# Attention's side work dealt by counts, its output product on VectorE, and 12 instead of 8 of 32 weight jobs in the MoE

## The chip, the cores and the metric

One core of a Trainium2 chip. The metric is the device time of one execution in microseconds.

## The reference, cut to what matters

```python
def _attn_ref(q, k, v, w1, b1, w2):          # q, k, v: 4 x 8 x 576 x 64
    scores = scale * np.matmul(q, k.transpose(0, 1, 3, 2))
    ...                                      # bias: 8 tables over (i, j), one a head, from a small net
    scores = scores + bias.transpose(2, 0, 1)[None, :, :, :]
    attn = np.exp(scores - np.max(scores, axis=-1, keepdims=True))
    attn = attn / (np.sum(attn, axis=-1, keepdims=True) + 1e-09)
    return np.matmul(attn, v)

def _moe_ref(x, w_in, w_out, a, b):          # x: 2304 x 512, w_in: 512 x 2048, w_out: 2048 x 512
    h = x @ w_in
    P = a[0] + a[1] * h + a[2] * h ** 2 + a[3] * h ** 3
    Q = 1.0 + np.abs(b[0]) * np.abs(h) + np.abs(b[1]) * h ** 2
    return (P / (Q + 1e-06)) @ w_out
```

The output of attention, with its heads side by side, is the x of the second part. The weights come as 64-bit floating point numbers.

## The kernel before

There are three stages, each written out as a Python loop; every engine runs its instructions in the order in which they are written.

**Bias.** 36 row groups make the bias tables and store them in DRAM.

**Attention.** A unit is a pair of heads and a batch entry: 16 units, of five steps each. Step c of a unit takes 128 rows of the queries for both heads (c = 0 to 3), or the last 64 rows of both together (c = 4). `step_a(i)` issues step i's scores (`e_qk`, TensorE, into two tiles of PSUM that are used in turn), then ScalarE's exponential for the second head of the step before, then transposes of the probabilities of two steps before (`e_tp`, `e_tail`; ScalarE copies them out of PSUM), then some keys of PV (`e_pv`), then VectorE's copy of the scores with bias and minimum (`e_ttr`, L349, called the masked copy here; it frees the scores' PSUM). PV of a unit is done in two halves of its queries; each half has five keys (four of 128 keys for both heads and a last one), which come into the list `fill` at places 1 and 4, counted by the unit of the step two behind. Before, a step takes three from `fill` where more than four are in it, and two otherwise. `e_pvout` copies a finished half out of PSUM. `load_rb` fetches the factors (one over the row sum, spread over partitions) from DRAM, and `e_norm`, the output product, multiplies a unit by them and stores it in DRAM (`xd`).

**Weight jobs.** TensorE multiplies in a 32-bit format that keeps fewer bits, so each weight is split into a high and a low part. 32 jobs (16 column blocks f of two matrices) do this: `load` (two DMAs of 512 KB, `wx` and `wy`), VectorE `mag`, `tail`, `sign`, `power`, `low`, ScalarE `rebias`, and `store` (two DMAs of 256 KB). `w_load` later reads the parts back into SBUF. Before, 24 jobs stand in a list `bg`, the load of the job after next behind each store, and `step_a` takes as many entries of it as keep it even over the steps: some 198 entries over 71 steps, 2.8 a step. The other 8 (`LATE = 4` blocks) run in the MoE.

**MoE.** 48 steps; step s has 384 tokens and 256 of the hidden columns, 24 matmuls for h (`mm1`) and, for step s - 2, 18 for the output (`mm2`). In between, ScalarE, GpSimd and VectorE form the rational function (`rat0`, `rat1`, `dv0` to `dv4`, `pl1`). The first half of the steps uses hidden columns 0 to 1023, the second half the rest, whose weights are read in at steps 20 to 25. `job(s, stage)` puts a weight job into every second step, from step `J0` on. h lies in the same two PSUM tiles as the scores did; `dv1` frees them. The output product of the last unit stands between the stages.

## Time and profile before

| | |
|---|---|
| median of 3 runs | 773.12 us (764.43 to 775.09) |
| profiled execution | 770.95 us |
| its span | 769.2 us |
| bias stage, up to about | 62 us |
| attention, up to about | 357 us |
| MoE | the rest |

The span is the time from the first to the last recorded instruction; the profiled execution has 1.8 us around it. Busy time of an engine is the sum of its recorded instructions; matmuls overlap, so a TensorE that is always busy may still be held up, and where it is shows in the time from one start to the next. Idle time is given with what ended it.

### The profile page before, as it was taken

Reading aid. Unit: us, or ns where it says so; the run is one execution under the profiler, and the core shown is the slowest. Engines: PE = TensorE matmul, PEld = TensorE weight load, DVE = VectorE, ACT = ScalarE, POOL = GpSimd, SP = SyncE. Lnnn points to the kernel's source line nnn. Section 1 sums busy time; section 2 is a strip of 40 time slices with the busy share of each in tenths; the row PEclk is TensorE's granted clock in tenths of the full one; section 3 lists DMA queues with packets and bytes.
Section 4 is the critical chain, followed back from the end, with each engine's and each line's share of the span. In section 5 each row is a group of like instructions: output and inputs, shape, how many; then the busy total and the mean of one; then the engine's idle time right before and its main releaser. Section 6 shows DMA issues by size and latency. Waiting matters only on the chain.

```text
span 769.2 us, 12185 instructions
## 1 busy us (share of the span) xinstructions
PE 738.1 (96%) x4210; PEld 561.5 (73%) x4210; DVE 572.2 (74%) x963; ACT 516.1 (67%) x965; POOL 204.3 (27%) x122
## 2 busy tenths in 40 slices
PE   6899999999999989999799999999999999999997
PEld 2236666655665656667788998998998899899896
DVE  7995766756667647563789999998776878687766
ACT  5978878766786767785657767666666656655552
POOL 0000000000000000000545444534533443443452
PEclk9999999989999999999999999999999999999999
DMA  4888788888879868954515263515853121230121
GB/s 135 295 289 280 233 278 273 294 274 268 272 251 286 273 226 285 302 181 138 179 43 164 83 193 111 188 69 171 237 187 117 42 82 52 72 124 17 65 83 41
DMA packets 107420, 137.66 MB, mean 179 GB/s; under 512 B 17104, under 2 KB 66528, under 8 KB 107360
## 3 DMA queue, kind: packets, MB, share of 16 engines
q1 hardware_dynamic: 106768, 136.11, 54.3%
q8 instruction: 33, 0.54, 0.3%
q10 hardware_dynamic: 592, 0.78, 0.3%
q14 instruction: 27, 0.22, 0.1%
HBM read 94.96 MB, written 41.90 MB: 178 GB/s over the span
## 4 chain that ended last, share of the span: by engine, by line
PE 79%; DMA 4%; DVE 3%; ACT 3%; issue 2%; POOL 1%; SPq 0%; DVEq 0%; POOLq 0%
PE o L749 26%; PE h L313 25%; PE sc L338 11%; PE tp L416 8%; PE pv L449 7%; PE pv L454 2%; DVE s L349 1%; DMA wx<-in_w_out_dram 1%; DMA k<-in_kt_dram 1%; ACT p L367 1%; PE pv L431 1%; DMA ws<-wh 1%; ACT ptm L511 1%; DVE wh L152 1%; DMA xr<-xd 0%
## 5 line engine op out<-in xcount | busy, mean ns | idle before, releaser
L679 POOL TENSOR_TENSOR u<-u,w 128x768 f32<-128x768 f32 x48 | 93.7, 1951 | 197.6 <-ACT u L677 189.1
L349 DVE CUSTOM_DVE_ANT_0 s<-sc,bias 128x576 f32<-128x576 f32 x144 | 103.7, 752 | 45.3 <-PE sc L338 40.4
L367 ACT ACTIVATE p<-s,m 128x576 f32<-128x576 f32 x144 | 112.8, 783 | 12.7 <-DVE m L349 12.4
L511 ACT COPY ptm<-tp 128x512 f32<-128x512 f32 x144 | 78.4, 588 | 58.6 <-PE tp L416 57.6
L400 POOL TENSOR_TENSOR xs<-xs,rb 128x576 f32<-128x576 f32 x16 | 23.6, 1473 | 341.7 <-DMA rb<-rs 191.3
L676 ACT ACTIVATE w<-h 128x768 f32<-128x768 f32 x48 | 39.1, 814 | 103.4 <-PE h L313 102.0
L338 PE MATMUL sc<-k,q 64*128 64x288 f32 x512 | 95.4, 442 | 11.0 <-DVE m L349 9.6
L313 PE MATMUL h<-xh,wg 128*128 128x384 f32 x384 | 102.6, 338 | 0.0
L718 POOL TENSOR_TENSOR gl<-m,r 128x768 fp32r<-128x768 f32 x47 | 87.2, 1854 | 13.7 <-DVE m L711 13.7
L338 PEld LDWEIGHTS sc<-k,q 64*128 64x128 f32 x512 | 51.2, 189 | 48.0 <-DVE m L349 23.5
L416 PEld LDWEIGHTS tp<-ident,p 128*128 128x128 f32 x576 | 65.5, 145 | 27.9 <-issue 8.9
L416 PE MATMUL tp<-ident,p 128*128 128x128 f32 x576 | 82.5, 286 | 0.0
L687 DVE TENSOR_TENSOR t<-t,h 128x768 f32<-128x768 f32 x48 | 45.7, 952 | 46.0 <-ACT t L678 28.1
L749 PE MATMUL o<-wg,gh 128*128 128x512 f32 x288 | 79.0, 391 | 0.0
L449 PE MATMUL pv<-ptm,v 128*64 128x320 f32 (+1 forms) x512 | 77.9, 427 | 0.0
L683 ACT ACTIVATE r<-u,qc 128x768 f32<-128x768 f32 x48 | 45.1, 940 | 42.6 <-POOL u L679 42.6
L313 PEld LDWEIGHTS h<-xh,wg 128*128 128x128 f32 x384 | 70.5, 190 | 1.1
L711 DVE SCALAR_TENSOR_TENSOR m<-t,cst,m 128x768 f32<-128x768 f32 x48 | 64.1, 1336 | 1.7
L313 PE MATMUL h<-xh,wih 128*128 128x384 f32 x192 | 64.9, 338 | 0.0
L313 PE MATMUL h<-xl,wg 128*128 128x384 f32 x192 | 64.8, 338 | 0.0
L313 PE MATMUL h<-xh,wil 128*128 128x384 f32 x192 | 64.7, 337 | 0.0
L313 PE MATMUL h<-xl,wih 128*128 128x384 f32 x192 | 64.6, 336 | 0.0
(77 smaller groups left out, 1390.6 us busy)
## 6 DMA issues: line engine op xcount, KB each, us to landing
tab<-e SPq DMA_DIRECT2D x36, 295.5 KB
wx<-in_w_in_dram SPq DMA_DIRECT2D x16, 512.0 KB
wy<-in_w_in_dram SPq DMA_DIRECT2D x16, 512.0 KB
wx<-in_w_out_dram SPq DMA_DIRECT2D x16, 512.0 KB
wy<-in_w_out_dram SPq DMA_DIRECT2D x16, 512.0 KB
ws<-wh SPq DMA_DIRECT2D x32, 256.0 KB
ws<-wl SPq DMA_DIRECT2D x32, 256.0 KB
wg<-ws SPq DMA_DIRECT2D x32, 256.0 KB
```

Of the source, the lines that this page charges most:

```text
L313: T.matmul(hps[s][:, j, :TT], w[:, k, sl], x[:, k, :], start=(k == 0 and z == 0), stop=(k == KD - 1 and z == 2),)
L338: T.matmul(sc[i, j][:, a, :SH], l, k[r, o + a * SH:o + (a + 1) * SH], start=True, stop=True,)
L349: V.tensor_tensor_reduce(out=t.rearrange("p (a s) -> p a s", a=2), in0=sc.pop((i, j))[:, :, :SH], in1=bias[p][:, idx, :].rearrange("p (a s ...
L367: A.activation(out=prob[i][:, z * S:z * S + S], in_=t, func=AF.Exp, bias=m, scale=-1.0, accum_out=ssum[u][:, k:k + 1],)
L416: T.transpose(ps[:, kc, :], prob[i][:, k0:k0 + P], ident)
L449: T.matmul(ps[64 * j:64 * j + 64, :w], v[:, kc, 64 * j:64 * j + 64], ptm[u, hf][:, kc, j, :w], start=(kc == 0), stop=False,)
L511: A.copy(out=o, in_=x)
L679: G.tensor_tensor(out=u, in0=u, in1=w, op=ALU.mult)
L687: V.tensor_tensor(out=rt[s, "t"], in0=rt[s, "t"], in1=hps[s][:, :, :TT], op=ALU.mult)
L711: V.scalar_tensor_tensor(out=m, in0=rt[s, "t"], scalar=abs_[:, 0:1], in1=m, op0=ALU.add, op1=ALU.subtract)
L718: eng.tensor_tensor(out=lo, in0=rt[s, "m"], in1=rt[s, "r0"], op=ALU.mult)
L749: T.matmul(po[n, c], l[:, j, c * P:(c + 1) * P], r[fp][:, j, :], start=(first and x is a), stop=(last and x is z),)
```

## The change

In attention each step takes a fixed number of PV keys (`PV_KEYS`) and of VectorE's job instructions (`JOB_OPS`), by its place in the unit two steps behind. The list of a job's entries is made anew (`in_order`): the load of the job after next stands behind `sign`, and `rebias` is put aside (`actq`) and issued early in ScalarE's part of the next step. The reciprocal of the row sums stands behind the masked copies, and `e_pvout` behind the jobs. The output product moves from GpSimd to VectorE and, for units 0 to 14, from place 3 of the next unit to place 0 of the one after it. In the MoE `LATE = 6` leaves 12 jobs, one every second step as before, from step 1 on; 20 stay in attention. Their order is changed so that both blocks of a pair come together.

```diff
@@ -75,7 +75,7 @@
     wih, wil, woh, wol = {}, {}, {}, {}
     wide = w_in.dtype != F32
     KH = KF // 2
-    LATE = 4
+    LATE = 6
 
     def w_alloc(pool, g):
         for d_, nm in ((wih, "wih"), (wil, "wil")):
@@ -193,14 +193,16 @@
     def w_job(f, part):
         return w_conv(f, part) if wide else w_plain(f, part)
 
-    def ahead(jobs, after=()):
-        seq = [j[0] for j in jobs[:2]]
-        for i, (_, *stages) in enumerate(jobs):
-            for st in stages:
-                seq += st
+    def in_order(jobs, after):
+        seq = [("sp", j[0]) for j in jobs[:2]]
+        for i, (_, first, act, last) in enumerate(jobs):
+            *vec, store = last
+            seq += [("dve", x) for x in first[:1]] + [("act", x) for x in act]
+            seq += [("dve", x) for x in first[1:] + vec[:1]]
             if i + 2 < len(jobs):
-                seq.append(jobs[i + 2][0])
-            seq += after.get(i, [])
+                seq.append(("sp", jobs[i + 2][0]))
+            seq += [("dve", x) for x in vec[1:]] + [("sp", store)]
+            seq += [("sp", x) for x in after.get(i, [])]
         return seq
 
     def w_hilo(f, part):
@@ -397,7 +399,7 @@
             def e_norm(u):
                 x = xs.pop(u)
                 p, b = units[u]
-                G.tensor_tensor(out=x, in0=x, in1=rb.pop(u), op=ALU.mult)
+                V.tensor_tensor(out=x, in0=x, in1=rb.pop(u), op=ALU.mult)
                 nc.sync.dma_start(out=xd[b][:, p, :], in_=x)
 
             def half(c):
@@ -473,6 +475,22 @@
             fill = []
             NU = len(units)
             TL = 2
+            PV_KEYS = (2, 3, 1, 2, 2)
+            JOB_OPS = (1, 2, 2, 1, 1)
+            actq = []
+
+            def run_act():
+                while actq:
+                    actq.pop(0)()
+
+            def run_jobs(n):
+                while bg and (n > 0 or bg[0][0] != "dve"):
+                    kind, fn = bg.pop(0)
+                    if kind == "act":
+                        actq.append(fn)
+                    else:
+                        fn()
+                    n -= kind == "dve"
 
             def step_a(i):
                 def ok(d):
@@ -502,21 +520,22 @@
                 if ok(1):
                     for j in heads(i - 1)[1:]:
                         e_exp(i - 1, j)
-                    if steps[i - 1][1] == 4:
-                        e_recip(steps[i - 1][0])
+                run_act()
                 if ok(TL):
                     hs = heads(i - TL)
                     for j in hs:
                         for o, x in e_tp(i - TL, j):
                             A.copy(out=o, in_=x)
                     tails, fin = e_tail(i - TL)
-                for _ in range((3 if len(fill) > 4 else 2) if i < NS + TL else len(fill)):
+                for _ in range(PV_KEYS[(i - TL) % 5] if i < NS + TL else len(fill)):
                     if fill:
                         e_pv(*fill.pop(0))
                 if ok(0):
                     for j in heads(i):
                         e_ttr(i, j)
                     e_exp(i, heads(i)[0])
+                if ok(1) and steps[i - 1][1] == 4:
+                    e_recip(steps[i - 1][0])
                 if ok(TL):
                     for o, x in tails:
                         A.copy(out=o, in_=x)
@@ -533,15 +552,14 @@
                     w_load(KH - 1, 0)
                 if i == NS + 1:
                     load_x(1, 1)
-                want = min(2, max(0, i - 3)) if i < 5 else 2 + (i - 4) * (nbg - 2) // (NS - 9)
-                e_pvout()
                 u2, c2 = divmod(i - TL, 5)
+                if c2 == 0 and 1 < u2 <= NU:
+                    e_norm(u2 - 2)
                 if c2 == 0 and 0 < u2 <= NU:
                     load_rb(u2 - 1)
-                if c2 == 3 and 0 < u2 <= NU:
-                    e_norm(u2 - 1)
-                while bg and nbg - len(bg) < want:
-                    bg.pop(0)()
+                if i >= 2:
+                    run_jobs(JOB_OPS[c2] if i >= 3 else 0)
+                e_pvout()
 
             with ExitStack() as bctx:
                 tpool = bctx.enter_context(tc.tile_pool(name="tpool", bufs=1, side="right"))
@@ -595,11 +613,10 @@
                     after[2 * (f + 2) + 1] = [lambda f=f: [w_load(f, z) for z in range(2)]]
                 for f in range(4, 6):
                     after[2 * f + 5] = [lambda f=f: [w_load(f, z) for z in range(2)]]
-                after[18] = [lambda: w_carve(1)]
+                after[16] = [lambda: w_carve(1)]
                 for f in range(2, 4):
-                    after[18 + f] = [lambda f=f: [w_load(f, z) for z in range(2)]]
-                bg = ahead(bg, after)
-                nbg = len(bg)
+                    after[15 + f] = [lambda f=f: [w_load(f, z) for z in range(2)]]
+                bg = in_order(bg, after)
 
                 for n in range(LEAD):
                     relu(n)
@@ -651,7 +668,8 @@
             for i in range(EARLY, NS + TL + 1):
                 step_a(i)
             while bg:
-                bg.pop(0)()
+                run_act()
+                run_jobs(1)
             while fill:
                 e_pv(*fill.pop(0))
             e_pvout()
@@ -778,8 +796,10 @@
 
             for f in range(KH - 2, KH):
                 w_load(f, 1)
-            jobs = [w_job(f, y) for f in range(KF - LATE, KF) for y in range(2)]
-            J0 = FPR
+            jobs = [
+                w_job(f + j, y) for f in range(KF - LATE, KF, 2) for y in range(2) for j in range(2)
+            ]
+            J0 = 1
             for x in jobs[:2]:
                 x[0]()
```

The lines of the changed kernel are up to 20 further down (L338 is L340, L349 is L351, L400 is L402, L687 is L705). In the rows below the number in a name is the step (`sc31_0`: scores of step 31, head 0) or the unit (`pv5_0`: PV of unit 5, half 0), and the last number only tells buffers apart.

TensorE's queue in attention, from the scores of step 31 to those of step 32 (`tp29` and `tt29` are the transposes of step 29), before:

```order
L338 MATMUL sc31_0_1982<-k6_1752,q6_1751 128x288
L338 MATMUL sc31_1_1983<-k6_1752,q6_1751 128x288
L338 MATMUL sc31_0_1982<-k6_1752,q6_1751 128x288
L338 MATMUL sc31_1_1983<-k6_1752,q6_1751 128x288
L416 MATMUL tp29_2_1989<-ident_60,p29_1922 128x128 x4
L434 MATMUL tt29_1995<-ident_60,p29_1922 128x128
L435 MATMUL tt29_1995<-ident_60,p29_1922 64x128
L378 MATMUL tt29_1995<-ident_60,sum5_1735 9x128
L338 MATMUL sc32_0_2024<-k6_1752,q6_1751 128x288
L338 MATMUL sc32_1_2025<-k6_1752,q6_1751 128x288
```

and now:

```order
L340 MATMUL sc31_0_1965<-k6_1737,q6_1736 128x288
L340 MATMUL sc31_1_1966<-k6_1737,q6_1736 128x288
L340 MATMUL sc31_0_1965<-k6_1737,q6_1736 128x288
L340 MATMUL sc31_1_1966<-k6_1737,q6_1736 128x288
L418 MATMUL tp29_2_1972<-ident_60,p29_1903 128x128 x4
L436 MATMUL tt29_1978<-ident_60,p29_1903 128x128
L437 MATMUL tt29_1978<-ident_60,p29_1903 64x128
L380 MATMUL tt29_1978<-ident_60,sum5_1726 9x128
L451 MATMUL pv5_0_1807<-ptm5_0_1793,v5_1561 64x256 x2
L456 MATMUL pv5_0_1807<-ptl5_0_1794,vdg2_109 128x256
L340 MATMUL sc32_0_2007<-k6_1737,q6_1736 128x288
L340 MATMUL sc32_1_2008<-k6_1737,q6_1736 128x288
```

Between the transposes of step 29 and the scores of step 32 now stand the last two keys of half 0 of unit 5; before there were none.

VectorE's queue in steps 32 and 33 (the masked copies, L139 to L163 job instructions, the copy of PV `xs5_`), before:

```order
L349 ISA s2_32_1_2056,m32_1_2057<-sc32_1_2025,bias1_783 128x576
L349 ISA m32_1_2057 128x1
L139 TENSOR_SCALAR wk4_1_2067<-wx4_1_1882 128x512
L147 TENSOR_SCALAR wm4_1_2069<-wy4_1_1883 128x512
L349 ISA s2_33_0_2096,m33_0_2097<-sc33_0_2073,bias1_783 128x576
L349 ISA m33_0_2097 128x1
L349 ISA s2_33_1_2099,m33_1_2100<-sc33_1_2074,bias1_783 128x576
L349 ISA m33_1_2100 128x1
L467 COPY xs5_1965<-pv5_1_1911 128x320
L152 SCALAR_TENSOR_TENSOR wh4_1_2071<-wx4_1_1882,wh4_1_2071 128x512
L158 TENSOR_SCALAR wk4_1_2067<-wh4_1_2071 128x512
L163 SCALAR_TENSOR_TENSOR wl4_1_2108<-wm4_1_2069,wk4_1_2067 128x512
```

and now:

```order
L351 ISA s2_32_1_2039,m32_1_2040<-sc32_1_2008,bias1_795 128x576
L351 ISA m32_1_2040 128x1
L402 TENSOR_TENSOR xs4_1780<-xs4_1780,rb4_1824 128x576
L147 TENSOR_SCALAR wm4_0_2052<-wy4_0_1733 128x512
L351 ISA s2_33_0_2079,m33_0_2080<-sc33_0_2054,bias1_795 128x576
L351 ISA m33_0_2080 128x1
L351 ISA s2_33_1_2082,m33_1_2083<-sc33_1_2055,bias1_795 128x576
L351 ISA m33_1_2083 128x1
L152 SCALAR_TENSOR_TENSOR wh4_0_2014<-wx4_0_1732,wh4_0_2014 128x512
L158 TENSOR_SCALAR wk4_0_1999<-wh4_0_2014 128x512
L469 COPY xs5_2001<-pv5_1_1896 128x320
L351 ISA s2_34_2_2119,m34_2_2120<-sc34_2_2097,bias1_795 128x576
```

Step 32 has the product of unit 4 (L402) and one job instruction where two stood; step 33 has two with the copy of PV behind them, where the copy and then three stood.

VectorE's queue at the passage to the MoE (`t0`, `gh0` and `m0` are of MoE step 0: `dv0`, `dv1`, `dv2`, `dv3`, `dv4`), before:

```order
L467 COPY xs15_4135<-pv15_0_4006 128x256
L467 COPY xs15_4135<-pv15_1_4084 128x320
L687 TENSOR_TENSOR t0_4239<-t0_4239,h0_4117 128x768
L690 SCALAR_TENSOR_TENSOR t0_4239<-t0_4239,cst_61,h0_4117 128x768
L299 TENSOR_TENSOR xl1_4248<-xr1_4167,xh1_4247 128x384
L697 SCALAR_TENSOR_TENSOR gh0_4254<-t0_4239,cst_61,r00_4251 128x768
L704 SCALAR_TENSOR_TENSOR m0_4256<-u0_4240,qc_65,gh0_4254 128x768
L711 SCALAR_TENSOR_TENSOR m0_4256<-t0_4239,cst_61,m0_4256 128x768
L687 TENSOR_TENSOR t1_4260<-t1_4260,h1_4187 128x768
L690 SCALAR_TENSOR_TENSOR t1_4260<-t1_4260,cst_61,h1_4187 128x768
```

and now:

```order
L469 COPY xs15_4098<-pv15_1_4016 128x320
L402 TENSOR_TENSOR xs15_4098<-xs15_4098,rb15_4111 128x576
L705 TENSOR_TENSOR t0_4171<-t0_4171,h0_4046 128x768
L708 SCALAR_TENSOR_TENSOR t0_4171<-t0_4171,cst_61,h0_4046 128x768
L301 TENSOR_TENSOR xl1_4180<-xr1_4095,xh1_4179 128x384
L715 SCALAR_TENSOR_TENSOR gh0_4186<-t0_4171,cst_61,r00_4183 128x768
L722 SCALAR_TENSOR_TENSOR m0_4188<-u0_4172,qc_65,gh0_4186 128x768
L729 SCALAR_TENSOR_TENSOR m0_4188<-t0_4171,cst_61,m0_4188 128x768
L705 TENSOR_TENSOR t1_4192<-t1_4192,h1_4119 128x768
L708 SCALAR_TENSOR_TENSOR t1_4192<-t1_4192,cst_61,h1_4119 128x768
L139 TENSOR_SCALAR wk10_0_4202<-wx10_0_4162 128x512
L147 TENSOR_SCALAR wm10_0_4204<-wy10_0_4163 128x512
```

The product of unit 15 (L402) stands ahead of `dv0`; before it stood ahead of GpSimd's first product of the MoE. Behind `dv1` of step 1 now stand the first two instructions of a job.

## Rows read from the trace of the kernel before

**Rows 1.** The page's busy time of the engines: microseconds, share of the span, number of instructions.
```profile
PE 738.1 (96%) x4210; PEld 561.5 (73%) x4210; DVE 572.2 (74%) x963; ACT 516.1 (67%) x965; POOL 204.3 (27%) x122
```

**Rows 2.** Busy time by stretches of the span: three of attention, one of the MoE's first half (steps with weight jobs in them), one of its later steps without. The columns are the stretch, its length, then busy time and number of instructions of each engine, the granted clock of TensorE as a share of full speed, the mean busy share of the 16 DMA engines, and GB/s.
```profile
120.00:180.00 60.00, 58.05 (x360) 36.65 (x360) 37.59 (x94) 43.97 (x113) 4.49 (x3) 0.94 0.83 273
180.00:240.00 60.00, 58.35 (x379) 36.48 (x378) 40.19 (x100) 44.75 (x114) 4.47 (x3) 0.97 0.85 271
240.00:300.00 60.00, 55.58 (x339) 34.64 (x336) 35.68 (x88) 41.79 (x106) 5.50 (x4) 0.94 0.84 263
...
398.00:465.00 67.00, 67.00 (x339) 60.69 (x339) 62.20 (x69) 44.32 (x59) 30.75 (x17) 1.00 0.44 140
...
532.00:599.00 67.00, 67.00 (x339) 60.69 (x339) 48.97 (x49) 42.71 (x56) 29.86 (x17) 1.00 0.54 171
```

**Rows 3.** The transposed row sums (L378), one a unit of attention: durations in ns, then the first and the last start in us.
```profile
L378 PE MATMUL tt<-ident,sum x16: 272/272/273, 75.8 to 356.8; 128*9 128x128 f32 x16
```

**Rows 4.** Timeline of TensorE over one unit of attention. The columns, here and in the other timelines: start in us, duration in us, engine, line, operation, out<-in, shape, number of instructions (weight loads left out, the records of a matmul's passes counted); in brackets, where the engine was idle before, for how long and what released it.
```profile
207.60 0.27 PE L378 MATMUL tt<-ident,sum 128*9 128x128 f32 x1
207.81 1.91 PE L338 MATMUL sc<-k,q 64*128 64x288 f32 x8
209.66 1.10 PE L416 MATMUL tp<-ident,p 128*128 128x128 f32 x8
210.59 0.27 PE L431 MATMUL pv<-ident,p 128*128 128x128 f32 x1
...
221.99 0.65 PE L449 MATMUL pv<-ptm,v 128*64 128x256 f32 x4
222.57 0.70 PE L454 MATMUL pv<-ptl,vdg 128*128 128x256 f32 x2
223.20 1.24 PE L338 MATMUL sc<-k,q 64*128 64x288 f32 x8
224.37 0.66 PE L416 MATMUL tp<-ident,p 128*128 128x128 f32 x4
...
225.08 0.27 PE L378 MATMUL tt<-ident,sum 128*9 128x128 f32 x1
225.58 1.19 PE L338 MATMUL sc<-k,q 64*128 64x288 f32 x4 [0.22 <-DVE m L349]
```

**Rows 5.** Timeline of VectorE at the end of the same unit: the masked copies of two heads.
```profile
224.76 0.75 DVE L349 CUSTOM_DVE_ANT_0 s<-sc,bias 128x576 f32<-128x576 f32 x1
225.44 0.75 DVE L349 CUSTOM_DVE_ANT_0 s<-sc,bias 128x576 f32<-128x576 f32 x1
```

**Rows 6.** Timelines of TensorE, VectorE and GpSimd around three places of attention; the row at 220.50 is the same VectorE instruction at a quiet place.
```profile
164.73 0.27 PE L378 MATMUL tt<-ident,sum 128*9 128x128 f32 x1
166.69 2.96 PE L338 MATMUL sc<-k,q 64*128 64x288 f32 x8 [1.68 <-DVE m L349]
...
187.01 0.27 PE L378 MATMUL tt<-ident,sum 128*9 128x128 f32 x1
...
163.35 1.42 DVE L152 SCALAR_TENSOR_TENSOR wh<-wx,wh 128x512 uint32<-128x512 uint32 x1
...
186.12 1.85 DVE L152 SCALAR_TENSOR_TENSOR wh<-wx,wh 128x512 uint32<-128x512 uint32 x1
...
220.50 0.69 DVE L152 SCALAR_TENSOR_TENSOR wh<-wx,wh 128x512 uint32<-128x512 uint32 x1 [2.26 <-ACT wh L144]
...
241.95 1.85 DVE L152 SCALAR_TENSOR_TENSOR wh<-wx,wh 128x512 uint32<-128x512 uint32 x1
...
186.02 1.41 POOL L400 TENSOR_TENSOR xs<-xs,rb 128x576 f32<-128x576 f32 x1 [21.80 <-DMA rb<-rs]
```

**Rows 7.** From the chain of waits (first row: start, length, what), and the timelines of VectorE and TensorE, around the weight tile that came late.
```profile
281.15 6.73 DMA wx<-in_w_out_dram
...
287.91 0.43 DVE L139 TENSOR_SCALAR wk<-wx 128x512 uint32<-128x512 uint32 x1 [5.54 <-DMA wx<-in_w_out_dram]
...
289.07 2.87 PE L338 MATMUL sc<-k,q 64*128 64x288 f32 x8 [2.51 <-DVE m L349]
```

**Rows 8.** Groups of instructions by line: over the whole span, over attention (60 to 345), and over the MoE's steps with jobs (398 to 535). The columns behind the count are busy us, mean ns of one, and idle time before them with its releasers.
```profile
L687 DVE TENSOR_TENSOR t<-t,h 128x768 f32<-128x768 f32 x48 | 45.7, 952 | 46.0 <-ACT t L678 28.1 <-PE o L749 17.9
...
L299 DVE TENSOR_TENSOR xl<-xr,xh 128x384 fp32r<-128x384 f32 x2 | 1.1, 554 | 0.0
...
L152 DVE SCALAR_TENSOR_TENSOR wh<-wx,wh 128x512 uint32<-128x512 uint32 x8 | 13.6, 1704 | 0.0
```

**Rows 9.** Timelines at the passage from attention to the MoE: ScalarE, GpSimd, VectorE, TensorE, and the queue of SyncE.
```profile
361.60 1.03 ACT L677 ACTIVATE u<-w,babs 128x768 f32<-128x768 f32 x1 [1.50 <-DMA xr<-xd]
...
365.69 1.61 POOL L400 TENSOR_TENSOR xs<-xs,rb 128x576 f32<-128x576 f32 x1 [15.19 <-DVE t L690]
367.26 1.84 POOL L679 TENSOR_TENSOR u<-u,w 128x768 f32<-128x768 f32 x1
...
363.54 0.95 DVE L687 TENSOR_TENSOR t<-t,h 128x768 f32<-128x768 f32 x1 [0.78 <-ACT t L678]
...
372.12 0.51 PE L749 MATMUL o<-woh,gh 128*128 128x512 f32 x1 [1.53 <-DVE gh L697]
377.67 2.16 PE L749 MATMUL o<-woh,gl 128*128 128x512 f32 x6 [2.47 <-POOL gl L718]
...
369.63 0.43 SPq L127 DMA_DIRECT2D wx<-in_w_in_dram  x1
```

## The prediction

> **What bounds the kernel now.** I read the engines' busy time first, then the table by stretches, then the timeline of single units. TensorE is busy 96% of the span [rows 1]. By stretches it splits in two. In the MoE it is busy 67.00 of 67.00 us at full clock, with weight jobs in the steps (398 to 465) and without (532 to 599): TensorE is the bound there, and VectorE, at 62.20 of 67.00, comes close only where jobs run [rows 2]. In attention TensorE shows 55.6 to 58.4 of 60, ScalarE 41.8 to 44.8, VectorE 35.7 to 40.2, the DMA engines 0.83 to 0.85, and the granted clock is below 1.00 in all three stretches [rows 2]. So nothing is saturated there, and TensorE is held up by something that comes and goes.
>
> A unit of attention is five steps; the transposed row sums (L378) mark it once. 16 marks from 75.8 to 356.8 make 281.0 / 15 = 18.73 us a unit [rows 3]. A quiet unit takes 225.08 - 207.60 = 17.48 [rows 4]. That leaves two questions: what is lost in a quiet unit, and what the other 281.0 - 15 x 17.48 = 18.8 us are.
>
> **Lost in every unit.** The four scores matmuls at 223.20 need 224.37 - 223.20 = 1.17 us; the same at 207.81, right behind the step with one head's transposes, need 1.85, and before the like group at 225.58 TensorE is idle again [rows 4]. Scores write the PSUM tiles that VectorE's masked copy (L349) of the step before has still to read: those run from 224.76 to 225.44 + 0.68 (their spacing) = 226.12 [rows 5], while TensorE has only some 0.8 us of transposes to do meanwhile (224.37 to 225.08, and the last one). That is 0.68 + 0.1 of waiting, 0.75 taken.
>
> **Lost now and then.** VectorE's sign instruction (L152), 0.69 us when alone at 220.50, takes 1.42 at 163.35 and 1.85 at 186.12 and 241.95; GpSimd's output product (L400) runs from 186.02, over the second of them. The masked copies queue behind, TensorE is idle 1.68 us, and after that idle time its scores take 2.96 instead of 1.17 [rows 6]: the granted clock, 0.94 over 120 to 180, means some 7 us at 1.2 of 2.4 GHz [rows 2]. The units that end at 187.01 and 207.60 cost 22.28 and 20.59 [rows 6, 4], 4.8 and 3.1 more than the quiet one; the third collision I price like the second: 11.0 in all. Another stall is a load: VectorE waits 5.54 us for a weight tile that was issued at 281.15 and took 6.73, and TensorE idles 2.51 us behind it [rows 7].
>
> The Trainium skill has this ("GPSIMD Engine Reference", section 1, Specifications): GpSimd shares its SBUF interfaces with VectorE, in contention with VectorE instructions that have two SBUF inputs or run in a two-port mode. The rows on the sign instruction agree. The same sentence speaks against the other half of the change, since it moves jobs to the MoE, where GpSimd works all the time; by it a job is dearer there, which would cost time only if VectorE were the bound.
>
> **The change part by part.**
>
> *PV keys.* Ten keys a unit, before as 3, 2, 3, 2, 0 over its five steps, now 2, 3, 1, 2, 2. The step that had none gets two: 223.20 - 221.99 = 1.21 us [rows 4]. Its cover becomes 0.8 + 1.21 = 2.0 us against the 1.75 (224.37 to 226.12) that the masked copies needed: the wait is gone. The step that falls to one key has one head's scores: one masked copy (0.8 us) behind 0.93 of transposes and a key of 0.58. No new wait there. Gain 14 x 0.75 = 10.5 us (the last unit has no scores behind it). Bounds: nothing if the wait moves to another step; 11.8 if all 0.84 goes.
>
> *Output product on VectorE, two steps later.* The 16 products leave GpSimd, which then does nothing in attention: the 11.0 go. On VectorE one 576-wide product lies between 0.554 (384 wide) and 0.952 (768 wide) [rows 8], 0.75 in proportion, in a step whose two masked copies and one job instruction leave it a microsecond; it hides behind TensorE's 3.4 us. Its factors were loaded a unit before, so it doesn't wait, but for the last (below). Queued behind it are job instructions and the copy out of PV's PSUM.
>
> *Jobs by number, 20 rather than 24.* Every step gets 1 or 2 VectorE job instructions, ScalarE's a step later, and the row sums' reciprocal stands behind the masked copies: this takes waits off the head of VectorE's queue, and costs nothing while VectorE has a third of its time free. The loads: one is issued behind the sign, and seven VectorE instructions, five steps or 17 us, lie before its use; before it was eight of 2.8 a step, some 10 us. Against 6.73 us of landing that is 10 us of slack where there were 3. Four jobs of 1.5 MB less take 6 of some 76 MB (the stage's 283 us at 269 GB/s [rows 2]) off the queue. Of the remaining 18.8 - 11.0 = 7.8 us of excess I take 4; bounds 0 and 7.8. Added: x for the MoE now loads one step behind the store that it reads, not three, with SP standing still for some 5 us and row sums and v behind it; ScalarE's first cast comes three steps later, about when x lands. I take 0, bounds 0 and 3 us.
>
> *The passage to the MoE.* GpSimd's last product waits for its factors until 365.69, and the MoE's first product u, whose input ScalarE finished at 361.60 + 1.03 = 362.6, stands behind it until 367.26. TensorE then idles 1.53 + 2.47 = 4.0 us [rows 9]. With the product on VectorE, u runs 4.6 us earlier, but VectorE's first two MoE instructions wait behind the product until 365.69 + 0.75 = 366.4 instead of starting at 363.54, and the third group of h matmuls needs the PSUM that they free: about 2 us of new idle time. The first job now starts in step 1, its load (issued 369.63 [rows 9], landing 6 to 7 us later) at the head of VectorE's queue, 1 to 2 us late. Net gain 2; bounds -1 and 4.
>
> *Four more jobs in the MoE.* Four jobs cost VectorE 62.20 - 48.97 = 13.2 us in 67 (8 steps) [rows 2]; the sign instruction is the dear one, 1.70 there [rows 8]. The 8 added job steps look like those at 398 to 465: VectorE keeps 4.8 us free, TensorE waits for nothing. Cost 0, hidden by TensorE; without this cover 13.
>
> **The rivals.** *The queue holds the pace (754).* DMA at 0.83 to 0.85 with big loads of 6 us: if loads stay as late as before, the unit goes to about 17.6 rather than 16.9, and 770.95 - 16 - 1 = 754. For it: the one stall seen at 281; against it: it is one in 16 units. *The even deal only moves the wait (759).* Then only collisions (11) and little else go: 759. Against it: every step's cover is over what the masked copies need. *Slower (790).* The job's first instruction heads VectorE's queue, with the masked copies behind it and TensorE behind those, as at 287.91 [rows 7]. If SP runs more than 17 - 7 = 10 us behind the program, each of 20 jobs waits. The gains are used up at 27 / 20 = 1.4 us a job, and past 2.1 us the kernel is over 2% slower; at 2.3 it is 771 - 27 + 46 = 790. For it: SP is in order, and its waits for stores are kept; against it: the slack grew.
>
> *VectorE falls behind in the MoE (757).* GpSimd works beside it in every step, a sign instruction takes 1.70 us, and 12 jobs over 24 steps leave no stretch of the first half in which VectorE could catch up: the 13 us above then come back, 744 + 13 = 757. For it: 93% busy; against it: the rows with jobs at full TensorE, and VectorE's work per step isn't raised. The skill's sentence above is the rule that would bring this about.
>
> **How the numbers follow.** Profiled execution 770.95 (span 769.2 and 1.8 around it), 2.2 under the median of 773.12: 770.95 - 10.5 - 11 - 4 + 0.5 for new small waits - 2 = 744. Its own range is 737 to 752, 0.68; the queue 0.13; the moved wait 0.08; the MoE 0.05; slower 0.06. All bounds together (11.8 + 18.8 + 4) give 736; the range 735 to 759 leaves out the slower case and the outer part of the moved wait. 2% of the median, about what a measurement of this kernel can tell from no change, is 757.7: faster 0.80, same 0.14, slower 0.06.
>
> **What would show it.** Right: marks of L378 about 16.9 apart and a sum near 254 for 15; scores after the short step back at 1.17; sign instructions at 0.69 throughout attention and no GpSimd instruction there; granted clock 1.00; the MoE unchanged at 8.4 us a step. Wrong: VectorE's weight instructions waiting for wx; scores waiting in another step; idle TensorE in MoE steps 1 to 4 or 20 to 24; a wait of ScalarE for x before the last steps.

## The result, and the profile after

The changed kernel takes 747.23 us (median of 4 runs, 745.69 to 751.96) against 773.29 for the one before, measured beside it: a ratio of 0.972, 95% interval 0.967 to 0.977. The profiled execution took 745.69 us, with a span of 743.9, 25.3 less than before. One of the 10 runs of `b_even` (775.73 us) and one of the 4 of `a_oldlist` (1167.75 us, at a granted clock of 0.56) were in a slower state, and the table below leaves them out. The page's busy times now [rows 1]:

```profile
PE 723.1 (97%) x4210; PEld 550.7 (74%) x4210; DVE 581.7 (78%) x979; ACT 514.9 (69%) x965; POOL 184.5 (25%) x106
```

By stretches, with the columns of [rows 2]. Attention's last mark comes 23.2 us earlier, so the first three stretches hold a little more of it:

```profile
120.00:180.00 60.00, 59.39 (x403) 37.36 (x403) 40.24 (x106) 48.25 (x124) 0.00 (x0) 1.00 0.80 258
180.00:240.00 60.00, 60.00 (x410) 37.28 (x408) 41.49 (x108) 48.40 (x126) 0.00 (x0) 1.00 0.88 285
240.00:300.00 60.00, 60.00 (x410) 37.74 (x408) 40.38 (x107) 48.97 (x126) 0.00 (x0) 1.00 0.89 282
398.00:465.00 67.00, 67.00 (x339) 60.69 (x338) 65.33 (x69) 44.74 (x59) 32.00 (x16) 1.00 0.42 143
532.00:599.00 67.00, 67.00 (x339) 60.69 (x338) 58.05 (x60) 41.88 (x54) 31.95 (x17) 1.00 0.44 146
```

In these stretches of attention TensorE is busy but for 0.61 us, and its granted clock is 1.00. In the MoE VectorE went from 62.20 to 65.33 of 67 and TensorE still misses nothing. The marks, as in [rows 3]:

```profile
L380 PE MATMUL tt<-ident,sum x16: 272/273/273, 78.7 to 333.6; 128*9 128x128 f32 x16
```

15 units take 254.9 us instead of 281.0. One unit in TensorE's timeline, from mark to mark (columns of [rows 4]):

```profile
198.02 0.27 PE L380 MATMUL tt<-ident,sum 128*9 128x128 f32 x1
198.22 0.65 PE L451 MATMUL pv<-ptm,v 128*64 128x256 f32 x4
198.80 0.70 PE L456 MATMUL pv<-ptl,vdg 128*128 128x256 f32 x2
199.43 1.24 PE L340 MATMUL sc<-k,q 64*128 64x288 f32 x8
200.60 1.09 PE L418 MATMUL tp<-ident,p 128*128 128x128 f32 x8
...
214.96 0.27 PE L380 MATMUL tt<-ident,sum 128*9 128x128 f32 x1
```

214.96 - 198.02 = 16.94: the scores behind the short step take 1.17 (199.43 to 200.60), not 1.85. Of the 0.68 won there a unit keeps 0.53. The other 0.15 is in the keys of one half, which stand in three places now instead of two (TensorE's timelines, before, then after):

```profile
218.24 1.52 PE L449 MATMUL pv<-ptm,v 128*64 128x256 f32 x12
219.68 1.24 PE L338 MATMUL sc<-k,q 64*128 64x288 f32 x8
...
209.18 0.65 PE L451 MATMUL pv<-ptm,v 128*64 128x256 f32 x4
209.76 1.24 PE L340 MATMUL sc<-k,q 64*128 64x288 f32 x8
...
212.07 1.08 PE L451 MATMUL pv<-ptm,v 128*64 128x256 f32 x8
213.08 1.24 PE L340 MATMUL sc<-k,q 64*128 64x288 f32 x8
```

Three keys in one go took 219.68 - 218.24 = 1.44; one and two take 0.58 + 1.01 = 1.59. Fourteen of the 15 units last 16.95, one 17.63, where k came 0.61 us late. Since 281.0 = 15 x 17.48 + 18.8 and 254.9 = 15 x 16.95 + 0.6, the quiet units gave 8.0 us and the irregular part 18.2.

Two other places moved. Before the first mark 2.9 us were lost (78.7 against 75.8); the timelines of VectorE and TensorE there:

```profile
69.27 0.43 DVE L139 TENSOR_SCALAR wk<-wx 128x512 uint32<-128x512 uint32 x1 [2.42 <-DMA wx<-in_w_in_dram]
70.78 0.43 DVE L147 TENSOR_SCALAR wm<-wy 128x512 uint32<-128x512 uint32 x1 [1.08 <-DMA wy<-in_w_in_dram]
71.12 0.75 DVE L351 CUSTOM_DVE_ANT_0 s<-sc,bias 128x576 f32<-128x576 f32 x1
...
71.93 1.23 PE L340 MATMUL sc<-k,q 64*128 64x288 f32 x6 [2.21 <-DVE m L351]
```

The first job's two instructions now come so early that VectorE waits for their loads with a masked copy behind them, and TensorE behind that; in the 3.4 us from 73.70 on its granted clock is 0.50. At the passage to the MoE the time from the last mark to the end fell from 412.4 to 410.3 (timelines of VectorE, GpSimd and TensorE, to be held against [rows 9]):

```profile
342.44 0.76 DVE L402 TENSOR_TENSOR xs<-xs,rb 128x576 f32<-128x576 f32 x1 [1.72 <-DMA rb<-rs]
343.12 0.95 DVE L705 TENSOR_TENSOR t<-t,h 128x768 f32<-128x768 f32 x1
...
340.67 1.84 POOL L697 TENSOR_TENSOR u<-u,w 128x768 f32<-128x768 f32 x1 [338.64 <-DMA xr<-xd]
...
345.26 0.41 PE L315 MATMUL h<-xh,wih 128*128 128x384 f32 x1 [0.89 <-DVE t L708]
...
376.72 0.50 PE L767 MATMUL o<-wg,gl 128*128 128x512 f32 x1 [0.91 <-POOL gl L736]
```

u runs at once, VectorE's first MoE instruction waits for the product, and TensorE idles 0.89 + 0.91 where it idled 1.53 + 2.47.

### The profile page after: what moved, and what is told of

Same layout as the page of the kernel before. It is cut to its first block, busy times and chain, and to the rows that moved or that the text cites. A ratio compares the mean times of both kernels' runs of the same rounds, so it can differ in the third digit from the quotient of the medians.

```text
span 743.9 us, 12201 instructions
## 1 busy us (share of the span) xinstructions
PE 723.1 (97%) x4210; PEld 550.7 (74%) x4210; DVE 581.7 (78%) x979; ACT 514.9 (69%) x965; POOL 184.5 (25%) x106
## 4 chain that ended last, share of the span: by engine, by line
PE 86%; DMA 5%; DVE 3%; SPq 2%; ACT 2%; issue 1%; POOL 0%; DVEq 0%; ACTq 0%; POOLq 0%
PE o L767 25%; PE h L315 24%; PE sc L340 11%; PE pv L451 9%; PE tp L418 9%; PE pb L633 4%; PE pv L456 3%; DMA wy<-in_w_in_dram 2%; ACT e L642 2%; DMA wy<-in_w_out_dram 1%; PE pv L433 1%; DMA k<-in_kt_dram 1%; DMA tab<-e 1%; DMA cst<-in_cst_dram 0%; DVE m L722 0%
## 5 line engine op out<-in xcount | busy, mean ns | idle before, releaser
L697 POOL TENSOR_TENSOR u<-u,w 128x768 f32<-128x768 f32 x48 | 96.7, 2015 | 475.2 <-DMA xr<-xd 338.6
L351 DVE CUSTOM_DVE_ANT_0 s<-sc,bias 128x576 f32<-128x576 f32 x144 | 104.0, 755 | 76.4 <-PE sc L340 74.1
L340 PE MATMUL sc<-k,q 64*128 64x288 f32 x512 | 82.6, 430 | 4.3 <-DVE m L351 2.6
L418 PEld LDWEIGHTS tp<-ident,p 128*128 128x128 f32 x576 | 63.1, 141 | 26.7 <-issue 11.5
L451 PE MATMUL pv<-ptm,v 128*64 128x320 f32 (+1 forms) x512 | 80.4, 425 | 0.0
L418 PE MATMUL tp<-ident,p 128*128 128x128 f32 x576 | 79.8, 280 | 0.0
L340 PEld LDWEIGHTS sc<-k,q 64*128 64x128 f32 x512 | 45.7, 187 | 37.3 <-issue 7.9
L722 DVE SCALAR_TENSOR_TENSOR m<-u,qc,gh 128x768 f32<-128x768 f32 x48 | 66.0, 1375 | 5.4 <-DVE gh L715 0.5
L705 DVE TENSOR_TENSOR t<-t,h 128x768 f32<-128x768 f32 x48 | 45.5, 948 | 26.7 <-ACT t L696 15.8
L715 DVE SCALAR_TENSOR_TENSOR gh<-t,cst,r 128x768 fp32r<-128x768 f32 x48 | 56.5, 1176 | 8.2 <-ACT r L702 5.8
```

Of the source, the lines that this page charges most:

```text
L340: T.matmul(sc[i, j][:, a, :SH], l, k[r, o + a * SH:o + (a + 1) * SH], start=True, stop=True,)
L351: V.tensor_tensor_reduce(out=t.rearrange("p (a s) -> p a s", a=2), in0=sc.pop((i, j))[:, :, :SH], in1=bias[p][:, idx, :].rearrange("p (a s ...
L418: T.transpose(ps[:, kc, :], prob[i][:, k0:k0 + P], ident)
L451: T.matmul(ps[64 * j:64 * j + 64, :w], v[:, kc, 64 * j:64 * j + 64], ptm[u, hf][:, kc, j, :w], start=(kc == 0), stop=False,)
L697: G.tensor_tensor(out=u, in0=u, in1=w, op=ALU.mult)
L715: V.scalar_tensor_tensor(out=hi, in0=rt[s, "t"], scalar=abs_[:, 0:1], in1=rt[s, "r0"], op0=ALU.add, op1=ALU.mult,)
```

## The experiments

All numbers of marks and units below are from the marks of one profiled execution of each kernel; medians and ratios (to the kernel before on the same chip) are from the timed runs. "The list" is the order and the dealing of job entries.

| kernel | median us | ratio, 95% interval | first mark | 15 units | last mark to end |
|---|---|---|---|---|---|
| before | 769 to 773 | 1 | 75.8 | 281.0 | 412.4 |
| `b_even` | 768.6 | 0.997 (0.994-1.001) | 74.8 | 282.1 | 411.2 |
| `b_prod` | 770.3 | 1.000 (0.997-1.003) | 75.6 | 277.8 | 415.2 |
| `b_even_prod` | 768.0 | 0.997 (0.993-1.001) | 74.8 | 269.9 | 417.1 |
| `b_pace` | 767.8 | 0.998 (0.994-1.001) | 77.7 | 273.2 | 412.5 |
| `a_24` | 759.2 | 0.987 (0.980-0.994) | 79.4 | 266.6 | 410.0 |
| `a_24f` | 764.3 | 0.994 (0.992-0.997) | 77.8 | 275.7 | 409.0 |
| `a_oldlist` | 750.7 | 0.973 (0.968-0.978) | 74.5 | 264.1 | 411.5 |
| `a_oldpv` | 754.9 | 0.979 (0.976-0.983) | 79.7 | 261.7 | 411.2 |
| `a_gps` | 749.6 | 0.971 (0.966-0.976) | 79.0 | 258.8 | 412.7 |
| `a_lead10` | 748.9 | 0.973 (0.967-0.979) | 78.1 | 257.2 | 410.8 |
| after, again | 746.8 | 0.971 (0.968-0.974) | 78.0 | 255.7 | 410.4 |
| `a_best` | 742.6 | 0.965 (0.963-0.968) | 75.4 | 255.0 | 410.2 |

**One part alone, on the kernel before: the even deal.**

```diff
-for _ in range((3 if len(fill) > 4 else 2) if i < NS + TL else len(fill)):
+for _ in range(PV_KEYS[(i - TL) % 5] if i < NS + TL else len(fill)):
```

> The kernel before with the even deal of PV keys alone (2, 3, 1, 2, 2). Theory (prediction's terms add up): the quiet unit falls from 17.48 to about 16.75 us, the collisions of GpSimd's product with VectorE stay; 10.5 us less, about 762.5. Rival A (one cover for both): a collision costs time only where TensorE's cover in the short step is missing; with the deal even, most of the 11 us of collisions go too, 18 to 21 us less, about 753. Rival B (the wait moves to the step with one key): marks stay about 17.5 apart in quiet units and the time stays within 3 us of before.

No gain in time, and by the profile none of the three: the quiet units are at 16.95, so the wait didn't move, yet four units take 19.3 to 27.3. VectorE, SyncE's queue and TensorE at the two longest:

```profile
179.13 0.43 DVE L139 TENSOR_SCALAR wk<-wx 128x512 uint32<-128x512 uint32 x1 [5.11 <-DMA wx<-in_w_in_dram]
260.33 0.43 DVE L139 TENSOR_SCALAR wk<-wx 128x512 uint32<-128x512 uint32 x1 [7.07 <-DMA wx<-in_w_out_dram]
...
173.95 0.45 SPq L127 DMA_DIRECT2D wx<-in_w_in_dram  x1
...
255.87 0.58 SPq L127 DMA_DIRECT2D wx<-in_w_out_dram  x1
...
180.56 2.96 PE L338 MATMUL sc<-k,q 64*128 64x288 f32 x8 [3.10 <-DVE m L349]
261.49 2.96 PE L338 MATMUL sc<-k,q 64*128 64x288 f32 x8 [4.38 <-DVE m L349]
```

The loads are late because they are issued late: VectorE stands idle from 179.13 - 5.11 = 174.02, the load is issued at 173.95 and lands 5.2 us later; the other lands 4.5 us after its issue. What the quiet units save is given back in the long ones. That TensorE, running ahead, meets the late loads sooner fits this, but no run isolates it.

**The product alone on VectorE, on the kernel before.**

```diff
-G.tensor_tensor(out=x, in0=x, in1=rb.pop(u), op=ALU.mult)
+V.tensor_tensor(out=x, in0=x, in1=rb.pop(u), op=ALU.mult)
...
-if c2 == 3 and 0 < u2 <= NU:
-    e_norm(u2 - 1)
+if c2 == 0 and 1 < u2 <= NU:
+    e_norm(u2 - 2)
```

> The kernel before with the output product alone on VectorE, two steps later. Theory (terms add up): quiet units stay at 17.48, the three units of 20.6 to 22.4 fall to 17.5, sign instructions show 0.69 in all of attention; 11 us less, and 2 more at the passage to the MoE, about 760. Rival A (one cover for both): the product itself takes 0.75 us of VectorE in a step, and without the even deal the cover is too short for that too, so that only 4 to 6 us are gained, about 768. Rival B (slower): VectorE's queue, 0.75 us fuller in a unit, is late for the masked copies in each of 15 units, about 778.

No gain either. GpSimd does nothing in attention now, but VectorE's waits for wx there have grown from 6.4 us in 3 places to (engine, waited for: us, times, longest):

```profile
DVE wk L139 <- DMA wx<-in_w_in_dram: 5.8, 3, 2.2
DVE wk L139 <- DMA wx<-in_w_out_dram: 5.6, 3, 3.2
```

The collisions are gone, and late loads take their place. The passage costs 2.8 more (415.2): `e_pvout` still stands ahead of the product here, as before, which puts the last products late, and TensorE waits for the MoE's first VectorE instructions behind them:

```profile
369.58 0.66 PE L313 MATMUL h<-xh,wih 128*128 128x384 f32 x1 [6.60 <-DVE t L690]
```

**Both together, with the old list** (the two edits above).

> The kernel before with the even deal of keys and the product on VectorE, with the old list of jobs. Theory P: loads are late here too, the more so since TensorE runs faster between two of them; quiet units at 16.95, but three to six units of 19 to 27 us, a time of 760 to 768. Rival S (the terms add up, 10.5 + 11 + 2): units at 17 nearly everywhere and a time near 747.

Theory P: 768.0. The sum of the two terms, 21.5 us, shows up as 11.1 in the units, and the passage takes 4.7 of it back. Its late loads hold VectorE for up to 4.6 us at a time.

**The product back on GpSimd, in the kernel after.**

```diff
-V.tensor_tensor(out=x, in0=x, in1=rb.pop(u), op=ALU.mult)
+G.tensor_tensor(out=x, in0=x, in1=rb.pop(u), op=ALU.mult)
```

> The kernel after with the output product put back on GpSimd at its new place; all else as after. Theory (terms add up): collisions return, three to five units show 19 to 22 us, and the passage loses the 2 us again; about 760. Rival A (one cover for both): a collision of about 1 us finds 2.0 us of TensorE's work ahead of it and costs nothing, so that only the passage's 2 us return and the time is 749.

Rival A, to the microsecond. The ratio can't be told from after's. Thirteen units are 16.95 with GpSimd's products of 1.4 us in them. The first of the other two waits for k, not for VectorE; the last unit (17.88) does wait behind a collision (timelines of TensorE and VectorE; VectorE's group of L163 in 62 to 330):

```profile
177.61 1.24 PE L340 MATMUL sc<-k,q 64*128 64x288 f32 x8 [2.03 <-DMA k<-in_kt_dram]
...
333.69 0.33 PE L433 MATMUL pv<-ident,p 128*128 128x128 f32 x1 [0.90 <-ACT ptl L541]
...
329.68 2.23 DVE L301 TENSOR_TENSOR xl<-xr,xh 128x384 fp32r<-128x384 f32 x2
```

```profile
L163 DVE SCALAR_TENSOR_TENSOR wl<-wm,wk 128x512 fp32r<-128x512 uint32 x20 | 14.7, 734 | 0.2
```

The collisions are still there (L163 takes 734 ns here, 679 with GpSimd idle): four of them cost VectorE 4 us over four lines in this stretch, and TensorE nothing. A fifth, with the MoE's x at 329.68 (2.23 us for two instructions that take 1.01 in after), costs it 0.90. The passage takes 2.3 more, as Rival A said.

**The old deal of keys, in the kernel after.**

> The kernel after with the old deal of PV keys (3 of more than four, else 2); all else as after. Theory (terms add up): the 0.75 us wait in the step without keys returns in 14 units, marks 17.5 to 17.7 apart, 757.5. Rival A (one cover for both): VectorE's product and the job instructions by number lie in a step whose cover is gone, so units of 18 us and more appear, 763 or above. Rival C (pacing did it): with jobs by number VectorE is never late and the wait doesn't return; 748.

The theory, at two thirds of its size: every unit but the last is 17.47 or 17.48, so the even deal is worth 0.53 a unit, 6.8 us in the units and 7.7 in the medians. No new wait joined it.

**The new list alone, on the kernel before** (`in_order`, `actq`, job instructions dealt 2, 2, 2, 1, 1 for 24 jobs, the places of the reciprocal and `e_pvout`).

> The kernel before with the new list of jobs alone: a fixed number of VectorE's job instructions in each step (2, 2, 2, 1, 1 for 24 jobs), the load of the job after next behind sign, rebias put aside, the reciprocal behind the masked copies; the old deal of keys, the product on GpSimd at its old place, 8 jobs in the MoE. Theory P (late loads are the irregular excess, and the new list removes them): units 17.48 nearly everywhere although GpSimd's product still runs, 15 units in 263 to 265 us, a time near 755. Rival S (the prediction's sum: 4 us for the list, 11 for GpSimd's collisions, which stay): units of 20 to 22 remain, a time near 767.

By the units P (13 of 15 at 17.48, with GpSimd's product in them and all signs at 0.68), by the time S. Two new waits eat the rest: k is 3.69 us late at 268, and ScalarE stands still 3.4 us for x ahead of 332 (TensorE's timeline):

```profile
268.25 2.29 PE L340 MATMUL sc<-k,q 64*128 64x288 f32 x8 [3.69 <-DMA k<-in_kt_dram]
332.38 2.35 PE L418 MATMUL tp<-ident,p 128*128 128x128 f32 x8 [1.57 <-ACT ptm L528]
```

**24 jobs in attention, in the kernel after** (with the parts read back where the kernel before does it).

```diff
-LATE = 6
+LATE = 4
-JOB_OPS = (1, 2, 2, 1, 1)
+JOB_OPS = (2, 2, 2, 1, 1)
-J0 = 1
+J0 = FPR
```

> The kernel after with 24 jobs in attention (2, 2, 2, 1, 1 instructions over the five steps) and the 8 old ones in the MoE, from step 4 on. Theory P: the loads keep some 13 us from issue to use, landing takes 5 to 6, so units stay at 16.95 and the time within 3 us of after. Rival Q (the DMA queues are full, and four jobs less are what lets the loads come in time): units of 18 and more return, 752 or above. Rival V (jobs are dear in the MoE): the MoE gets shorter by 2 to 5 us with four jobs less, a time of 742 to 744.

Rival Q's time; P falls. But wx isn't what is late. The same two places as in the run above hold TensorE (timelines of TensorE, ScalarE and SyncE's queue):

```profile
264.66 1.52 PE L340 MATMUL sc<-k,q 64*128 64x288 f32 x8 [4.01 <-DMA k<-in_kt_dram]
329.35 2.35 PE L418 MATMUL tp<-ident,p 128*128 128x128 f32 x8 [4.43 <-ACT ptm L528]
...
327.55 0.51 ACT L300 CAST xh<-xr 128x384 fp32r<-128x384 f32 x1 [6.62 <-DMA xr<-xd]
...
256.75 0.33 SPq L262 DMA_DIRECT2D k<-in_kt_dram  x1
...
321.81 0.58 SPq L289 DMA_DIRECT2D xr<-xd  x1
```

The mark at whose step this k is called for is at 248.8: SyncE issues it 7.9 us later, and the scores that need it start 7.9 us after that, 4.0 late. In after the largest such lag is 5.8 (the one unit of 17.63). x is issued at 321.81, the x of after at

```profile
307.65 0.58 SPq L289 DMA_DIRECT2D xr<-xd  x1
```

SyncE's issues stand in one queue. They take 0.52 us each on average, and in after 24 of them follow one another from 238.93 to 255.38 with no gap over 0.3. In the 8.4 us ahead of the late k here (248.37 to 256.75) SyncE makes 13 other issues, which take 6.9 us themselves; 1.5 us are gaps. The landing of wx is no longer than in after (where it is recorded, 4.4 us in the median against 4.9, 7.6 against 7.1 at most), and the DMA engines move less (260 GB/s in 240 to 300, 282 in after). So what four jobs less take away is, by the trace, the backlog of that queue. No run takes issues out of it and leaves the jobs, so this part is read, not shown. Rival V falls too: with four jobs less in the MoE the time behind the last mark is 0.3 us shorter.

**24 jobs, dealt faster** (2, 2, 2, 2, 1), so that they end ahead of the load of x.

> The kernel after with 24 jobs in attention as before, but dealt 2, 2, 2, 2, 1, so that the last ends some 8 steps earlier and the x of the MoE isn't loaded behind the last jobs' DMAs. Theory P2: ScalarE's wait for x (6.6 us) goes, the wait for k in unit 11 (4.0) stays or grows to 6 and one more may come, since SyncE has the same issues in fewer steps; 751 to 757. Rival E (only the crowded end made 24 jobs slow): both waits go, 747 to 749. Rival Q (DMA as a whole): no gain, 757 or above.

Rival Q's time, 764.3. The wait for x is gone, the wait for k is there five times, and a new one has come: `rebias` on ScalarE waits for earlier stores of wh, and TensorE waits behind it (waits of TensorE and ScalarE; TensorE's timeline at the longest):

```profile
PE sc L340 <- DMA k<-in_kt_dram: 9.1, 5, 3.2
...
ACT wh L144 <- DMA ws<-wh: 15.4, 7, 5.2
...
268.75 0.66 PE L418 MATMUL tp<-ident,p 128*128 128x128 f32 x4 [3.17 <-ACT ptm L528]
```

k is issued up to 9.7 us behind its mark. So it wasn't the crowded end alone that made 24 jobs slow, and the same issues in fewer steps make it worse.

**The old list with 20 jobs, in the kernel after.**

> The kernel after with the old list of jobs, dealt evenly over the steps by entries, still 20 jobs in attention; even deal, VectorE's product and the MoE as after. Theory P2 (what is late is SyncE's queue and the loads in it; four jobs less relieve both, the list only says how early a load is issued and whether VectorE waits on ScalarE): the lead from issue to use falls from 16 to some 10 us, two to four loads are late, units of 18 to 21 in a third of the places, 750 to 756. Rival N (only the number of jobs counts): units at 16.95 as after, 746 to 749. Rival L (only the list counts): as with 24 jobs and the old list, 760 or above.

At P2's lower end, and its runs, 747 to 752, reach into N's. P2's late loads don't come, though the lead from issue to use is 9.7 us on average: VectorE waits 0.5 us for wx in all. Seven units cost 0.15 to 0.45 more, where sign waits for ScalarE; one costs 7.5, since x comes late again (ScalarE's and TensorE's timelines):

```profile
319.97 0.51 ACT L298 CAST xh<-xr 128x384 fp32r<-128x384 f32 x1 [7.32 <-DMA xr<-xd]
...
321.77 2.35 PE L416 MATMUL tp<-ident,p 128*128 128x128 f32 x8 [4.97 <-ACT ptm L526]
```

Against that its first mark is 4.2 earlier. With 20 jobs the new list is worth 1 to 2 us by the ratios and 4 by the medians; with 24 it is worth 9 (`b_even_prod` against `a_24`). Four jobs less are worth 12 with the new list (`a_24` against after) and 17 with the old one (`b_even_prod` against this run; the two differ also in the places of the reciprocal and of `e_pvout`).

**A shorter lead in the kernel after.**

```diff
-            seq += [("dve", x) for x in first[1:] + vec[:1]]
-            if i + 2 < len(jobs):
-                seq.append(("sp", jobs[i + 2][0]))
+            if 0 < i < len(jobs) - 1:
+                seq.append(("sp", jobs[i + 1][0]))
+            seq += [("dve", x) for x in first[1:] + vec[:1]]
```

> The kernel after with each job's load issued later in the list, four VectorE instructions ahead of its use instead of seven: some 10 us from issue to use where there were 16. Nothing else changes. Theory P (lead decides): landing takes 5 to 6 us and up to 11 at times, so two to five of 20 jobs wait for wx by 1 to 4 us at the head of VectorE's queue, units of 18 to 21 appear, a time of 750 to 757. Rival R (the even number of instructions in a step is what counts, not the lead): units stay at 16.95, within 2 us of after.

Nearer to R than to the theory. The lead fell from 16.0 to 8.2 us on average, and VectorE waits for wx five times (VectorE's waits):

```profile
DVE wk L139 <- DMA wx<-in_w_out_dram: 6.7, 3, 4.8
DVE wk L139 <- DMA wx<-in_w_in_dram: 4.5, 2, 3.0
```

The wait of 3.0 is the one at the start, which after has too. Of the four others, 0.9 to 4.8 us, only the longest reaches TensorE (its timeline), and the units cost 2.3 more:

```profile
253.95 0.33 PE L433 MATMUL pv<-ident,p 128*128 128x128 f32 x1 [2.76 <-DVE xs L469]
```

With even keys and an even list waits of 0.9 to 1.5 us for a load are absorbed, and 2.0 of the 4.8. The 11 us to land that the expectation allows for are in no trace: no landing of wx on record takes more than 7.6.

**A version that beats both.** The first job instruction one step later (`i >= 4`), x of the second tile group loaded a step earlier, and the last unit's factors loaded ahead of the store before them.

> The kernel after with the first job instruction one step later, the x of the MoE's second tile group loaded a step earlier, and the factors of the last unit loaded ahead of the last but one product's store. Theory: the first mark comes at 76 to 76.5 instead of 78.7 (VectorE no longer waits at the head of its queue for the first wx and wy), and TensorE's 0.9 us wait for VectorE at the MoE's start shrinks; 2.5 to 3.5 us less than after. Rival: the jobs then end a step later and what was waiting at the start waits at the end; no difference.

742.6 (741.5 to 744.3) against 746.8 (745.9 to 748.9) of after on the same chip, 4.2 less. Its theory had 2.5 to 3.5. The first mark is at 75.4, 2.6 earlier than in the run beside it: the waits for wx and wy (1.37 and 1.09) now fall where TensorE has work. The passage didn't move (TensorE waits 0.82 in both). So 2.6 of the 3.5 us between the two profiled executions are the start; 0.7 are in the units, where k came 1.46 us late in the run beside it and 0.20 here.

## Why the prediction was right, and where it was not

The time (744 for 747) and the side were right, and the units, 255.5 by its terms, are 254.9. The split isn't what the runs show, and the sum came right partly by luck.

- **PV keys**: the mechanism held (scores at 1.17, the wait gone, no new one). The term was mis-sized: 0.53 a unit rather than 0.75, 6.8 to 8.0 us for 10.5. The wait itself was 0.68, and 0.15 of it went to the keys that now stand in three places, a cost that the prediction put at nothing. And it is worth this only where the loads keep up: alone it gave nothing.
- **Output product, 11 us of collisions**: this step failed. The collisions are real, but with the new list GpSimd's product costs TensorE 0.9 us in the last of 15 units and nothing in the others (`a_gps`; in `b_pace` no sign meets a product at all). The reading that fits is that the old list put sign where the masked copies were already waiting behind it; the even keys alone don't cover that (in `b_even` a sign of 1.83 at 277.11 still holds TensorE 1.13 us). The trace of before had a sign of 1.46 at 314.76 in a unit of 17.80: a collision, and no wait of TensorE. Taking the collisions away with the old list brought late loads (`b_prod`), and 3.2 us in the units for the 11. The prediction read the instruction that was long at the moment of the stall as its cause, and missed that another wait stood close behind.
- **Jobs by number, 20 rather than 24, 4 us**: the term that was far too small. The four jobs are worth 12 (`a_24`), the list 1 to 4 beside them. The prediction counted their bytes (6 of 76 MB) and the lead of wx; by the traces it is the issues in SyncE's queue ahead of k, of x and of the stores that come late. It had SyncE's backlog only in its slower rival, as a danger to wx.
- **The right sum**: 11 + 4 for the irregular part stood against 18.8 that were there, and 18.2 went. By the marks the quiet units gave 8.0 for 10.5, the irregular part 18.2 for 15, the passage 2.1 for 2, and the start took 2.9 where 0.5 stood for new small waits: 25.4 for 27. One term too large, one too small and one missing nearly cancel; that is luck, and it says nothing for the split.
- **Passage**: net 2, measured 2.1. VectorE's new wait for the factors is there as described; it costs TensorE 0.9 rather than 2, and 0.9 of the old idle time stays.
- **Four more jobs in the MoE**: nothing, as predicted; 67.00 of 67.00. The Trainium skill ("GPSIMD Engine Reference", section 1, Specifications) has GpSimd contend with VectorE instructions of two SBUF inputs. By it a job was to be dearer there; the trace agrees that someone pays, but not who. In 382 to 510 the sign instruction now takes 0.74 and the MoE's own product 1.63, which were 1.70 [rows 8] and, in the same stretch, 1.02 before:

```profile
L722 DVE SCALAR_TENSOR_TENSOR m<-u,qc,gh 128x768 f32<-128x768 f32 x16 | 26.1, 1631 | 1.7
...
L152 DVE SCALAR_TENSOR_TENSOR wh<-wx,wh 128x512 uint32<-128x512 uint32 x8 | 5.9, 738 | 0.0
```

- **x for the MoE, 0 of 0 to 3**: right for 20 jobs with the new list; ScalarE waits for it 3.4 us in `b_pace`, 6.6 in `a_24` and 7.3 in `a_oldlist`.
- **Not foreseen**: 2.9 us at the start. The prediction's slack of 10 us rests on a load that is seven VectorE instructions ahead. The first two jobs have no such lead: their loads are issued together at 65, and VectorE's first job instruction stands one step behind.
- **The rivals**: the queue does hold the pace with 24 jobs, but by late issues, not by loads that take 6 us. The wait didn't move, VectorE didn't fall behind in the MoE, and wx was late only at the start.

What stays open: at the late k of `a_24` SyncE's lag is mostly its own issues (6.9 of 8.4 us), but why one takes 0.3 us and another 1.5, and how much it had waited for others further back, no run separates. The smaller number of jobs wasn't tried alone on the kernel before.

## What to carry to other kernels

Where several waits take turns, removing one of them alone may give nothing: on the kernel before, the even keys, the product and the list, each alone, and the first two together, changed the time by 0.3% at most. Read the stall's cost from the spacing of marks, and its cause only from a run that takes it away. Where a load comes late, look at when it was issued before asking why it is slow. Count the DMA issues of one queue as you count instructions: a small load that is called for late in an in-order queue is late by all that stands before it.

## What the runs showed of the hardware

- SyncE's issues of a DMA take 0.52 us on average in attention. In after 24 of them, with gaps of at most 0.3 us, take 16.45 us.
- In `b_pace` 15 of GpSimd's products start between 89 and 343 us, and all 24 signs stay at 0.64 to 0.69 us: the same two instructions that collide in one order of a program never meet in another.
- It isn't sign alone that gets longer beside GpSimd's product: `tail` (L147, one input, 0.42 us) takes 1.66 at 85.55 in before and 1.44 at 266.99 in `a_gps`. The masked copy stays at 0.75 beside it (`b_pace` at 144.22).
- Idle time of TensorE is often, not always, followed by some microseconds at half the clock. After 4.38 us of idle time the scores took 2.96 us instead of 1.2 (`b_even`, at 261, granted clock 0.77 in 255 to 270); after 2.76 us in `a_lead10` at 254 the clock stayed at 1.00 in the whole stretch of 240 to 300.
